# Regrouping the first expert's matmuls by batch, and one weight transfer issued ahead of the last values

## Chip, cores, metric

One core of one Trainium2 chip runs the whole program. The metric is the device time of one execution in microseconds (us). "Before" is the tuned kernel, "after" the kernel with the change; every experiment was timed beside runs of the kernel before on the same chip (e1 to e8 on one chip, e9 and e10 on a second, e11 on a third). The engines go by their short names: PE does the matmuls (TensorE), ACT is ScalarE, DVE is VectorE, POOL is GpSimd, SPq the queue of the transfers that SyncE issues.

## The reference

A gated linear attention (4 batches, 8 heads, 768 steps, head size 48) feeds a mixture of four experts whose outputs are summed with the router's weights:

```python
for t in range(S):
    state = f[:, :, t, :, None] * state + k[:, :, t] (outer) v[:, :, t]
    y[:, :, t] = q[:, :, t] @ state
x = y as (batch * seq, heads * head_dim)            # 3072 x 384
for e in range(4):
    out += p[:, e:e+1] * (relu(x @ w1[e]) @ w2[e])  # w1 384x1024, w2 1024x384
```

## The kernel before

The 768 steps are cut into six chunks of 128; a chunk has 4 batches x 128 = 512 rows for the experts. Attention of the next chunk runs between the expert matmuls of this one. Nobody wrote the order of the instructions. The kernel describes each step as an `Op` with a cost, dependencies, a rank (`prio`, lower goes first) and the buffers it takes and frees. At build time a list scheduler, `Plan.run`, gives each free engine the best-ranked step that is ready, in a modelled time. Each engine then gets its instructions in the planned order and executes them in that order.

```python
rooms = {"ps_m": 4, "ps_t": 4, ..., "e": 3, ...}     # buffers of each kind; ps_* are PSUM banks, which matmuls write

def run(self):                                        # cut
    while left:
        for e in ("PE", "ACT", "DVE", "POOL", "DMA"):
            while free_at[e] <= now + 1e-9:
                # first step by rank that is ready and whose buffers are free
                ...
                for k in o.frees:
                    self.left[k] -= 1
                    if self.left[k] == 0:
                        freeing.append((o.end + self.LATENCY, k[0], self.slot[k]))
```

Three steps play a part later: the exponentials write the tile `e` (three buffers); for chunks after the first a small transfer `egs` copies one row of it elsewhere, and `e` is free once this copy and two products have read it; and loads for the chunk after next compete with transposing transfers (`tp`) on one queue.

```python
GS.append(P.add(f"egs {c}.{b}", {"POOL": 0.8}, on(dma_egs), s(10), deps=[ex], takes=[("egs", c, b)],
                frees=[("e", c, b)], lag=2.8) if c and more else None)
...
et = [P.add(f"tp {c}.{b}", {"DMA": 1.8}, on(dma_tp), s(4), deps=[qm, km], ...)]
...
add_load(c + 2, nm, 2 * half, 2, u0 + {0: 38}.get(c, 30) + 4 * half + j, deps=wd[3, 1])
...
if c == 0:                                            # expert 0 of the first chunk
    for fcs in (range(KF // 2), range(KF // 2, KF)):
        for n0, n1, xs in ((0, N2, LO), (N2, NT, HI)):
            zip_units([x for x in hl(c, 0, n0, n1, xs) if x[2] in fcs], [])
```

Of the kernel before, what the change touches and what calls it, by code (L numbers as in the profile page):

```python
# [102 lines left out]
def kernel(  # L103
# [11 lines left out]
    nc = tc.nc  # L115
    B, H, S, D = q.shape
    assert (B, H, S, D) == (4, 8, 768, 48)
    T = 128
# [6 lines left out]
    KD = Din // 128  # L125
    KF = F // 128
    NT = B * T
    N2 = NT // 2
# [11 lines left out]
    P = Plan(rooms)  # L140
# [18 lines left out]
    for i in range(rooms["e"]):  # L159
# [5 lines left out]
        out=mask01, in_=mask01, compare_op=ALU.is_ge, fill=0.0,  # L165
# [15 lines left out]
    w1_sb = wpool.tile([128, E, KD, F], BF16)  # L181
# [18 lines left out]
    def tl(kind, *key):  # L200

        if (kind, key) not in tiles:
            room = kind if kind in rooms else "ps_m" if kind in ("hp", "op", "pp") else "ps_t"
            slot = P.slot[(room, kind) + key if room.startswith("ps_") else (room,) + key]
            if room in ("gp", "qk", "e"):
                tiles[kind, key] = pads[room, slot]
            else:
                shape, dt = shapes[kind]
                pool = ps if room.startswith("ps_") else wk
                tiles[kind, key] = pool.tile(shape, dt, name=f"{room}{slot}")  # L210
        return tiles[kind, key]

    def after(later, earlier):
        tc.add_manual_dep(later.ins, earlier.ins.name,
                          mybir.DependencyInfo(mybir.DependencyClass.Sync, mybir.DependencyReason.DATA),
                          reason="order of transfers")
# [4 lines left out]
    def hh(b, n=1):  # L221
        return slice((b % 2) * H, (b % 2 + n) * H)
# [8 lines left out]
    def load(c, nm, b, n):  # L231
        if (c, nm) == (0, "v"):
            ins[c, nm, b] = nc.gpsimd.dma_start(out=tl("vb", c, b), in_=srcs[nm][c, :, b * H:(b + n) * H, :])  # L233
            if b < 2:
                after(ins[c, nm, b], ins[v_gate[b]])
            return
        ins[c, nm, b] = nc.sync.dma_start(out=tl(nm, c, b // 2)[:, hh(b, n), :],  # L237
                                          in_=srcs[nm][c, :, b * H:(b + n) * H, :])
        if (c, nm, b) == (1, "f", 0):
            after(ins[c, nm, b], ins["w", 6])  # L240
        if (c, nm, b) == (1, "f", 1):
            after(ins[c, nm, b], ins["w", w_gate])

    def load_w(i, e, which, ks, cols):
        w, r = (w1_sb, w1_r) if which == 1 else (w2_sb, w2_r)
        ins["w", i] = nc.gpsimd.dma_start(out=w[:, e, ks, cols], in_=r[e][:, ks, cols])  # L246
        if i == w_last:
            after(ins["w", i], ins[1, "k", 0])
# [115 lines left out]
        for kk in range(ks.start, ks.stop):  # L364
            nc.tensor.transpose(out=tl("xp", c, b, ks.start)[:, kk, :], in_=tl("yb", c, b)[:, kk * 128:(kk + 1) * 128], identity=ident)  # L365

    def mm_h(c, e, fc, n0, n1):
        for kk in range(KD):
            nc.tensor.matmul(out=tl("hp", c, e, fc, n0)[:, n0:n1], lhsT=w1_sb[:, e, kk, fc * 128:(fc + 1) * 128],  # L369
                             rhs=tl("xT", c)[:, kk, n0:n1], start=(kk == 0), stop=(kk == KD - 1))  # L370

    def half_of(c, n0):
        return n0 // N2 if c == 1 else 0

    def relu(c, e, fc, n0, n1, eng):
        dst, src = tl("h", c, e, half_of(c, n0))[:, fc, n0:n1], tl("hp", c, e, fc, n0)[:, n0:n1]
        if eng == "DVE":
            nc.vector.tensor_relu(out=dst, in_=src)  # L378
        else:
            nc.scalar.activation(out=dst, in_=src, func=AF.Relu)  # L380
# [21 lines left out]
    ld = {}  # L402
    def add_load(c, nm, b, n, prio, deps=(), cost=None):
        op = P.add(f"ld {nm}{c}.{b}", {"DMA": cost or (1.05 if c else 1.1) * n}, lambda e: load(c, nm, b, n), prio,
                   deps=deps, takes=[(nm, c, b // 2)], lag=2.0)
        for i in range(n):
            ld[c, nm, b + i] = op
        return op


    v_gate = [(0, "k", 1), (0, "k", 2)]
    for i, x in enumerate("f0 k0 q0 f1 k1 q1 f2 f3 k2 q2 v0 k3 q3 v1 v2 v3".split()):
        nm, b = x[0], int(x[1])
        if nm == "v":
            iss = P.add(f"v issue {b}", {"POOL": 0.8}, lambda _, b=b: load(0, "v", b, 1), -600 + b,
                        deps=[vi, ld[v_gate[min(b, 1)]]] if b else [ld[v_gate[0]]], takes=[("vb", 0, b)], lag=1.2)
            vi = iss
            ld[0, "v", b] = P.add(f"ld v0.{b}", {"DMA": 1.1}, lambda _: None, -1000 + i, deps=[iss], lag=2.0)
        else:
            add_load(0, nm, b, 1, -1000 + i)  # L420

# [4 lines left out]
    w_last, w_gate = len(pieces) - 1, len(pieces) - 3  # L426
    wd = {}
    for i, (e, which, ks, cols) in enumerate(pieces):
        if i == 7:
            add_load(1, "f", 0, 1, -454.5, deps=wd[2, 1], cost=0.1)  # L430
        if i == w_last:
            for x in ((1, "f", 1, 1), (1, "k", 0, 2), (1, "q", 0, 2), (1, "v", 0, 2)):
                add_load(*x, -430 + len(ld), deps=wd[3, 1])
        iss = P.add(f"w issue {i}", {"POOL": 0.8}, lambda _, i=i, x=(e, which, ks, cols): load_w(i, *x),
                    -500 + i, deps=[vi] + ([ld[1, "k", 0]] if i == w_last else []))
        op = P.add(f"w {i}", {"DMA": 2.25 if i < 6 else 4.5}, lambda _: None, -400 if i == w_last else -460 + i, deps=[iss], lag=1.5)
        wd[e, which] = wd.get((e, which), []) + [op]
    for x in ((1, "f", 2, 2), (1, "k", 2, 2), (1, "q", 2, 2), (1, "v", 2, 2)):
        add_load(*x, -400 + len(ld), deps=wd[3, 1])

# [95 lines left out]
    unit = [0]  # L536
    hdone, omm, oev = {}, {}, {}

    def add_h(c, e, fc, n0, n1, xs):
        p, n = unit[0], n1 - n0  # L540
        key = ("ps_m", "hp", c, e, fc, n0)
        m = P.add(f"h {c}.{e}.{fc}.{n0}", {"PE": 0.645 * n / NT}, lambda _: mm_h(c, e, fc, n0, n1), p,
                  deps=[wd[e, 1][fc * len(wd[e, 1]) // KF]] + [t for b in xs for t in xdone[c, b]], takes=[key], lag=0.2, frees=[("xT", c)])
        hdone[c, e, fc, n0] = P.add(f"relu {c}.{e}.{fc}.{n0}",
                                    {"ACT": 0.6, "DVE": 0.69} if n == NT else {"ACT": 0.39, "DVE": 0.42},
                                    lambda g: relu(c, e, fc, n0, n1, g), p - 3, deps=[m],
                                    takes=[("h", c, e, half_of(c, n0))], frees=[key])

    def add_o(c, e, nt, half):
        p = unit[0] + 0.5  # L550
# [20 lines left out]
    ALL, LO, HI = list(range(B)), [0, 1], [2, 3]  # L571

    def zip_units(hs, os):
        for i in range(max(len(hs), len(os))):
            if i < len(hs):
                add_h(*hs[i])
            if i < len(os):
                add_o(*os[i])
            unit[0] += 1

    def hl(c, e, n0, n1, xs):
        return [(c, e, fc, n0, n1, xs) for fc in range(KF)]

    def ol(c, e, nts):
        return [(c, e, nt, half) for nt in nts for half in range(2)]

    for c in range(C):
        u0 = unit[0]
        if c + 1 < C:
            base = u0 + {0: 10, 1: 0}.get(c, -6)  # L590
            attention(c + 1, lambda b, s, base=base: base + 2 + 5 * b + s, 2)
        if c + 2 < C:
            for half in range(2):
                for j, nm in enumerate("fkqv"):
                    add_load(c + 2, nm, 2 * half, 2, u0 + {0: 38}.get(c, 30) + 4 * half + j, deps=wd[3, 1])
        if c == 0:
            for fcs in (range(KF // 2), range(KF // 2, KF)):
                for n0, n1, xs in ((0, N2, LO), (N2, NT, HI)):
                    zip_units([x for x in hl(c, 0, n0, n1, xs) if x[2] in fcs], [])
        elif c == 1:  # L600
            zip_units([], ol(0, E - 1, ALL))
            zip_units(hl(c, 0, 0, N2, LO), [])
            for e in range(1, E):
                zip_units(hl(c, e, 0, N2, LO), ol(c, e - 1, LO))
            zip_units(hl(c, 0, N2, NT, HI), ol(c, E - 1, LO))
            for e in range(1, E):
                zip_units(hl(c, e, N2, NT, HI), ol(c, e - 1, HI))
            zip_units(hl(c + 1, 0, 0, NT, ALL), ol(c, E - 1, HI))
        elif c == 2:
            pass  # L610
        else:
            zip_units(hl(c, 0, 0, NT, ALL), ol(c - 1, E - 1, ALL))
        for e in range(E if c == 1 else 1, E):
            zip_units(hl(c, e, 0, NT, ALL), ol(c, e - 1, ALL))
# [3 lines left out]
    done = P.run()  # L618
# [45 lines left out]
```

## Time and profile before

| | before |
|---|---|
| time, median | 298.27 us (three runs, 298.17 to 299.92) |
| span of the profiled run | 296.4 us |
| PE waits from 25 us to the end | none |

The chain and PE's timeline around 20 us stand in the prediction.

### The profile page before, as it was taken

What the parts mean: (1) busy time and instruction counts of PE and PEld (TensorE: products, weight loads), DVE (VectorE), ACT (ScalarE), POOL (GpSimd) and SP (SyncE); (2) the same over time, 40 slices, a digit from 0 to 9 for tenths busy, and PEclk for the clock granted to TensorE, in tenths of its full rate; (3) what the DMA queues carried; (4) which work ended last, traced back from release to release, by engine and by line L of the source; (5) the groups of instructions that cost most, each with busy time, mean ns of one, the idle gap of its engine ahead of it and who ended that gap; (6) DMA issues with size and microseconds to landing.
All of it is one profiled execution on the core that took longest, in us unless ns stands there. A gap on an engine that the chain in (4) does not pass through costs nothing.

```text
span 296.4 us, 5570 instructions
## 1 busy us (share of the span) xinstructions
PE 289.8 (98%) x2161; PEld 170.7 (58%) x2161; DVE 127.8 (43%) x251; ACT 173.3 (58%) x318; POOL 107.8 (36%) x182
## 2 busy tenths in 40 slices
PE   7999999999999999999999999999999999999995
PEld 2467555567777775555555555555555555555553
DVE  6776012695674673055365435243523222101223
ACT  5757556757674677777475565554475544465440
POOL 5787201338578259145448372243220000000000
PEclk9999999999999999999999999999999999999999
DMA  7999999998989969996989942102521100200002
GB/s 149 201 154 206 207 194 197 182 200 184 189 174 193 183 136 203 206 209 119 196 163 209 175 96 32 29 0 67 123 59 31 27 2 27 80 2 0 0 2 106
DMA packets 136462, 36.43 MB, mean 123 GB/s; under 512 B 126812, under 2 KB 135644, under 8 KB 136436
## 3 DMA queue, kind: packets, MB, share of 16 engines
q1 hardware_dynamic: 125188, 29.35, 48.9%
q0 software_dynamic: 11248, 6.72, 16.5%
q8 instruction: 17, 0.28, 0.4%
q14 instruction: 9, 0.07, 0.1%
HBM read 31.51 MB, written 4.72 MB: 122 GB/s over the span
## 4 chain that ended last, share of the span: by engine, by line
PE 91%; DMA 4%; SPq 2%; POOL 1%; issue 0%; DVE 0%
PE ps_m L384 42%; PE ps_m L369 42%; DMA w_sb<-in_moe_w_dram 2%; SPq L237 2%; PE ps_t L325 2%; DMA k<-in_k_dram 1%; PE ps_t L340 1%; PE ps_t L336 1%; PE ps_t L346 1%; PE ps_t L273 1%; POOL vb L233 1%; PE ps_t L310 0%; POOL w_sb L246 0%; DVE o L391 0%; PE ps_t L365 0%
## 5 line engine op out<-in xcount | busy, mean ns | idle before, releaser
L380 ACT ACTIVATE h<-ps_m 128x512 bf16<-128x512 f32 (+1 forms) x191 | 101.9, 539 | 92.5 <-PE ps_m L369 89.1
L369 PE MATMUL ps_m<-xT,w_sb 128*128 128x512 bf16 (+1 forms) x696 | 152.1, 342 | 0.5 <-DMA w_sb<-in_moe_w_dram 0.5
L384 PE MATMUL ps_m<-w_sb,h 128*128 128x384 bf16 (+1 forms) x776 | 151.5, 324 | 0.0
L384 PEld LDWEIGHTS <-h 128*128 128x128 bf16 x776 | 75.1, 98 | 58.6
L391 DVE SCALAR_TENSOR_TENSOR o<-ps_m,pn,o 128x384 f32<-128x384 f32 (+1 forms) x73 | 44.6, 612 | 109.6 <-PE ps_m L384 103.3
L369 PEld LDWEIGHTS <-w_sb 128*128 128x128 bf16 x696 | 65.5, 98 | 43.3 <-DMA w_sb<-in_moe_w_dram 0.9
L301 POOL TENSOR_TENSOR qk<-q,e 128x384 bf16<-128x384 f32 x18 | 21.5, 1198 | 34.7 <-ACT e L293 32.4
L329 DVE TENSOR_TENSOR AT<-ps_t,mask 128x512 bf16<-128x512 f32 x48 | 29.9, 682 | 5.8 <-PE ps_t L325 5.8
L360 POOL TENSOR_TENSOR Sf<-Sf,egs 48x192 f32<-48x192 f32 x40 | 20.1, 501 | 33.1 <-DVE Sf L353 31.0
L293 ACT ACTIVATE e<-ps_t 128x384 f32<-128x384 f32 x48 | 26.7, 667 | 4.7 <-PE ps_t L273 3.5
L378 DVE TENSOR_SCALAR h<-ps_m 128x256 bf16<-128x256 f32 (+1 forms) x41 | 20.4, 508 | 19.0 <-PE ps_m L369 14.8
L301 POOL TENSOR_TENSOR qk<-k,e 128x384 bf16<-128x384 f32 x20 | 20.2, 1013 | 7.7 <-ACT e L293 4.4
L353 DVE TENSOR_TENSOR Sf<-Sf,ps_t 48x192 f32<-48x192 f32 x40 | 14.0, 350 | 10.9 <-PE ps_t L346 10.2
L246 POOL DMA_DIRECT2D w_sb<-in_moe_w_dram x11 | 8.8, 808 | 20.3 <-DMA k<-in_k_dram 19.0
L361 POOL CAST sb<-Sf 48x192 bf16<-48x192 f32 x40 | 13.6, 339 | 2.6
L393 ACT ACTIVATE o<-ps_m,pn 128x384 f32<-128x384 f32 x22 | 12.8, 581 | 2.8 <-PE ps_m L384 1.7
L629 PE MATMUL ps_m<-busy 128*128 128x512 bf16 x35 | 11.9, 449 | 1.5 <-DVE busy L144 1.5
L298 POOL DMA_DIRECT2D egs<-e x16 | 9.0, 564 | 7.7 <-ACT e L293 7.7
L265 ACT ACTIVATE ex<-f 128x768 f32<-128x768 f32 (+1 forms) x14 | 10.4, 745 | 2.1 <-DMA f<-in_f_logit_dram 2.0
L340 PE MATMUL ps_t<-vb,AT 128*128 128x48 bf16 x192 | 11.5, 184 | 0.0
L228 POOL CAST vb<-v 128x384 bf16<-128x384 f32 x18 | 9.7, 561 | 4.0 <-DMA v<-in_v_dram 3.8
L226 ACT CAST yb<-ps_t 128x384 bf16<-128x384 f32 (+1 forms) x14 | 6.5, 464 | 7.5 <-PE ps_t L340 7.3
(54 smaller groups left out, 126.7 us busy)
## 6 DMA issues: line engine op xcount, KB each, us to landing
out_dram<-o SPq DMA_DIRECT2D x23, 192.0 KB, 2.0
w_sb<-in_moe_w_dram POOLq DMA_DIRECT2D x5, 768.0 KB, 19.2
k<-in_k_dram SPq DMA_DIRECT2D x10, 384.0 KB, 5.4
q<-in_q_dram SPq DMA_DIRECT2D x10, 384.0 KB, 5.2
v<-in_v_dram SPq DMA_DIRECT2D x10, 384.0 KB, 5.3
f<-in_f_logit_dram SPq DMA_DIRECT2D x9, 384.0 KB, 5.0
w_sb<-in_moe_w_dram POOLq DMA_DIRECT2D x6, 384.0 KB, 9.0
f<-in_f_logit_dram SPq DMA_DIRECT2D x6, 192.0 KB, 3.7
```

The lines of the kernel that those rows point to most:

```text
L293: nc.scalar.activation(out=o, in_=i, func=AF.Exp, scale=1.0 if j else -1.0)
L301: engines[eng].tensor_tensor(out=tl("qk", c, b)[:, j, :, 0:D].rearrange("t (i r) d -> t i r d", r=2), in0=tl("qk"[j], c, b // 2)[:, hh(b), ...
L329: nc.vector.tensor_tensor(out=tl("AT", c, b)[:, r].rearrange("s i t -> s (i t)"), in0=tl("A", c, b, r).rearrange("s i t -> s (i t)"), in1= ...
L340: nc.tensor.matmul(out=y[:, h * D:(h + 1) * D], lhsT=AT[:, r, i, :], rhs=vb[:, h, :], start=(c == 0), stop=True, skip_group_check=True)
L353: nc.vector.tensor_tensor(out=Sf[rows, b], in0=Sf[rows, b], in1=KV[rows, :, r, :], op=ALU.add)
L360: nc.gpsimd.tensor_tensor(out=Sf[rows, b], in0=Sf[rows, b], in1=eg, op=ALU.mult)
L361: nc.gpsimd.tensor_copy(out=nb[rows, b, :, r * D:(r + 1) * D], in_=Sf[rows, b])
L369: nc.tensor.matmul(out=tl("hp", c, e, fc, n0)[:, n0:n1], lhsT=w1_sb[:, e, kk, fc * 128:(fc + 1) * 128], rhs=tl("xT", c)[:, kk, n0:n1], sta ...
L378: nc.vector.tensor_relu(out=dst, in_=src)
L380: nc.scalar.activation(out=dst, in_=src, func=AF.Relu)
L384: nc.tensor.matmul(out=tl("op", c, e, nt, part)[:, cols], lhsT=tl("h", c, e, half_of(c, nt * T))[:, fc, nt * T:(nt + 1) * T], rhs=w2_sb[:, ...
L391: nc.vector.scalar_tensor_tensor(out=o, in0=op, scalar=pe, in1=o, op0=ALU.mult, op1=ALU.add)
```

## The change

The intent is to give PE expert work earlier in the first 25 us: batch 2 no longer waits for batch 3, and the first weight piece no longer stands behind the values of batch 3. An F tile is 128 of the 1024 hidden columns of an expert. The diff, cut to its core (helpers that pass the number of F tiles in a bank, `nf`, are left out, and lines are shortened at `...`):

```diff
+    def hp(c, e, fc, n0, n1, nf):
+        return tl("hp", c, e, fc, n0)[:, 0:nf * (n1 - n0)].rearrange("p (f n) -> p f n", f=nf)
...
+    def add_v(b, prio):                       # issue of one batch's values, chained to the issue before it
+        issued.append(P.add(f"v issue {b}", ...))
-    for i, x in enumerate("f0 k0 q0 f1 k1 q1 f2 f3 k2 q2 v0 k3 q3 v1 v2 v3".split()):
+    for i, x in enumerate("f0 k0 q0 f1 k1 q1 f2 f3 k2 q2 v0 k3 q3 v1 v2".split()):
...
         iss = P.add(f"w issue {i}", ...)
+        issued.append(iss)
+        if i == 0:
+            add_v(B - 1, -459.5)              # values of batch 3 only after weight piece 0
...
         if c == 0:
-            for fcs in (range(KF // 2), range(KF // 2, KF)):
-                for n0, n1, xs in ((0, N2, LO), (N2, NT, HI)):
-                    zip_units([x for x in hl(c, 0, n0, n1, xs) if x[2] in fcs], [])
+            for fcs, n0, n1, xs, nf in ((range(0, KF // 2), 0, N2, LO, 1), (range(0, KF // 2, 2), N2, NT - T, [2], 2),
+                                        (range(KF // 2, KF), 0, NT - T, LO + [2], 1), (range(0, KF, 4), NT - T, NT, [3], 4)):
+                zip_units([(c, 0, fc, n0, n1, xs, nf) for fc in fcs], [])
+            unit[0] = u0 + 2 * KF
```

More of the change, by code (lines that the diff above doesn't have):

```diff
@@ L365, in pe_xt, with mm_h, relu @@
             nc.tensor.transpose(out=tl("xp", c, b, ks.start)[:, kk, :], in_=tl("yb", c, b)[:, kk * 128:(kk + 1) * 128], identity=ident)
-    def mm_h(c, e, fc, n0, n1):
-        for kk in range(KD):
-            nc.tensor.matmul(out=tl("hp", c, e, fc, n0)[:, n0:n1], lhsT=w1_sb[:, e, kk, fc * 128:(fc + 1) * 128],
-                             rhs=tl("xT", c)[:, kk, n0:n1], start=(kk == 0), stop=(kk == KD - 1))
+    def hp(c, e, fc, n0, n1, nf):
+        return tl("hp", c, e, fc, n0)[:, 0:nf * (n1 - n0)].rearrange("p (f n) -> p f n", f=nf)
+    def mm_h(c, e, fc, n0, n1, nf):
+        for f in range(nf):
+            for kk in range(KD):
+                nc.tensor.matmul(out=hp(c, e, fc, n0, n1, nf)[:, f], lhsT=w1_sb[:, e, kk, (fc + f) * 128:(fc + f + 1) * 128],
+                                 rhs=tl("xT", c)[:, kk, n0:n1], start=(kk == 0), stop=(kk == KD - 1))
     def half_of(c, n0):
         return n0 // N2 if c == 1 else 0
-    def relu(c, e, fc, n0, n1, eng):
-        dst, src = tl("h", c, e, half_of(c, n0))[:, fc, n0:n1], tl("hp", c, e, fc, n0)[:, n0:n1]
+    def relu(c, e, fc, n0, n1, nf, eng):
+        dst, src = tl("h", c, e, half_of(c, n0))[:, fc:fc + nf, n0:n1], hp(c, e, fc, n0, n1, nf)
         if eng == "DVE":
@@ L408, in add_load @@
         return op
-    v_gate = [(0, "k", 1), (0, "k", 2)]
-    for i, x in enumerate("f0 k0 q0 f1 k1 q1 f2 f3 k2 q2 v0 k3 q3 v1 v2 v3".split()):
+    v_gate, issued = [(0, "k", 1), (0, "k", 2)], []
+    def add_v(b, prio):
+        issued.append(P.add(f"v issue {b}", {"POOL": 0.8}, lambda _: load(0, "v", b, 1), -600 + b,
+                            deps=issued[-1:] + ([ld[v_gate[b]]] if b < 2 else []), takes=[("vb", 0, b)], lag=1.2))
+        ld[0, "v", b] = P.add(f"ld v0.{b}", {"DMA": 1.1}, lambda _: None, prio, deps=issued[-1:], lag=2.0)
+    for i, x in enumerate("f0 k0 q0 f1 k1 q1 f2 f3 k2 q2 v0 k3 q3 v1 v2".split()):
         nm, b = x[0], int(x[1])
         if nm == "v":
-            iss = P.add(f"v issue {b}", {"POOL": 0.8}, lambda _, b=b: load(0, "v", b, 1), -600 + b,
-                        deps=[vi, ld[v_gate[min(b, 1)]]] if b else [ld[v_gate[0]]], takes=[("vb", 0, b)], lag=1.2)
-            vi = iss
-            ld[0, "v", b] = P.add(f"ld v0.{b}", {"DMA": 1.1}, lambda _: None, -1000 + i, deps=[iss], lag=2.0)
+            add_v(b, -1000 + i)
         else:
@@ L434 @@
         iss = P.add(f"w issue {i}", {"POOL": 0.8}, lambda _, i=i, x=(e, which, ks, cols): load_w(i, *x),
-                    -500 + i, deps=[vi] + ([ld[1, "k", 0]] if i == w_last else []))
+                    -600 + 3 * i, deps=issued[-1:] + ([ld[1, "k", 0]] if i == w_last else []))
         op = P.add(f"w {i}", {"DMA": 2.25 if i < 6 else 4.5}, lambda _: None, -400 if i == w_last else -460 + i, deps=[iss], lag=1.5)
+        issued.append(iss)
         wd[e, which] = wd.get((e, which), []) + [op]
+        if i == 0:
+            add_v(B - 1, -459.5)
     for x in ((1, "f", 2, 2), (1, "k", 2, 2), (1, "q", 2, 2), (1, "v", 2, 2)):
@@ L537, with add_h @@
     hdone, omm, oev = {}, {}, {}
-    def add_h(c, e, fc, n0, n1, xs):
-        p, n = unit[0], n1 - n0
+    def add_h(c, e, fc, n0, n1, xs, nf=1):
+        p, n = unit[0], (n1 - n0) * nf
         key = ("ps_m", "hp", c, e, fc, n0)
-        m = P.add(f"h {c}.{e}.{fc}.{n0}", {"PE": 0.645 * n / NT}, lambda _: mm_h(c, e, fc, n0, n1), p,
+        m = P.add(f"h {c}.{e}.{fc}.{n0}", {"PE": 0.645 * n / NT}, lambda _: mm_h(c, e, fc, n0, n1, nf), p,
                   deps=[wd[e, 1][fc * len(wd[e, 1]) // KF]] + [t for b in xs for t in xdone[c, b]], takes=[key], lag=0.2, frees=[("xT", c)])
-        hdone[c, e, fc, n0] = P.add(f"relu {c}.{e}.{fc}.{n0}",
-                                    {"ACT": 0.6, "DVE": 0.69} if n == NT else {"ACT": 0.39, "DVE": 0.42},
-                                    lambda g: relu(c, e, fc, n0, n1, g), p - 3, deps=[m],
-                                    takes=[("h", c, e, half_of(c, n0))], frees=[key])
+        done = P.add(f"relu {c}.{e}.{fc}.{n0}",
+                     {"ACT": 0.6, "DVE": 0.69} if n == NT else {"ACT": 0.5, "DVE": 0.56} if n > N2 else {"ACT": 0.39, "DVE": 0.42},
+                     lambda g: relu(c, e, fc, n0, n1, nf, g), p - 3, deps=[m],
+                     takes=[("h", c, e, half_of(c, n0))], frees=[key])
+        for f in range(nf):
+            hdone[c, e, fc + f, n0] = done
     def add_o(c, e, nt, half):
```

## The prediction

> **What bounds the kernel now.** I read the page first. TensorE (PE) is busy 289.8 of 296.4 us, so only two things can shorten the run: less PE work, or less time in which PE waits or runs filler. I then read the chain of waits in order of time, to see where PE first becomes the whole chain.
>
> ```profile
> 14.55 0.70 POOL w_sb L246
> 15.25 7.25 DMA w_sb<-in_moe_w_dram
> 22.50 0.05 issue
> 22.54 0.50 PE ps_m L369 x3
> 23.04 0.34 PE ps_t L346 x8
> 23.38 0.66 PE ps_m L369 x6
> ...
> 25.03 4.24 PE ps_m L369 x30
> 29.27 1.30 PE ps_m L384 x8
> ```
>
> The columns are start, duration, what. Up to 22.50 the chain is a weight transfer; from 22.54 to the end it is PE. The list of PE's waits from 25 us to the end is empty. So the end moves by as much as the work that PE still has to do at about 22.5 us shrinks, or as that moment moves, and by nothing else. Which weight transfer is it? The timeline of PE around it:
>
> ```profile
> 18.76 0.36 PE L340 MATMUL ps_t<-vb,AT 128*128 128x48 bf16 x8
> 18.96 1.02 PE L629 MATMUL ps_m<-busy 128*128 128x512 bf16 x4
> 19.87 0.34 PE L365 MATMUL ps_t<-ident,yb 128*128 128x128 bf16 x3
> 20.05 0.36 PE L340 MATMUL ps_t<-vb,AT 128*128 128x48 bf16 x8
> 20.67 1.16 PE L369 MATMUL ps_m<-xT,w_sb 128*128 128x256 bf16 x9 [0.26 <-DMA w_sb<-in_moe_w_dram]
> 21.66 0.33 PE L365 MATMUL ps_t<-ident,yb 128*128 128x128 bf16 x3
> 21.83 0.49 PE L369 MATMUL ps_m<-xT,w_sb 128*128 128x256 bf16 x3
> 22.54 0.50 PE L369 MATMUL ps_m<-xT,w_sb 128*128 128x256 bf16 x3 [0.22 <-DMA w_sb<-in_moe_w_dram]
> ```
>
> Here L629 is filler (keeps PE active), L340 forms a batch's attention output y, L365 transposes it, L369 is the first MoE layer. At 20.67 PE waits for weight piece 0 (expert 0, F tiles 0 to 3); 12 matmuls (four F tiles by three K steps on batches 0 and 1) follow, and at 22.54 it waits again, for piece 1 (F tiles 4 to 7). Asking for each issue alone gave the landings: value transfers of batches 1, 2, 3 issued at 11.85, 12.8 and 13.7 landed near 15.5, 17.9 and 18.4; piece 0, issued at 14.5, took 6.1 us (20.6); piece 1, issued at 15.3, took 7.2 us (22.5); the next ones landed 1.9 to 2.0 us apart. The DMA engines show a busy share of one or more throughout, so this queue is limited by transfer, not by issue.
>
> **What the Trainium skill says.** "DMA: Bandwidth & Descriptors", section "Queues, rings and completion order", says that each DMA engine consumes one ring's descriptors in order, but that completion is not FIFO over the engines. The landings agree roughly: all in issue order, though batches 2 and 3 landed 0.5 us apart and batches 1 and 2 2.4 us apart, so what one transfer costs the next isn't a constant. "TensorE: Matmul & The Clock Gate", section "Back-to-back issue gap", gives about 81 ns per matmul at N=128 in a stream that loads weights each time, against 56 ns isolated. The new kernel has such a stream, so it matters. This trace decides for 56: transposes with a new 128x128 stationary operand each go at 0.45/8 = 56 ns,
>
> ```profile
> 56.84 0.45 PE ps_t L310 x8
> ```
>
> and the 256-column matmuls at 0.66/6 = 110 ns. "PSUM — Partial Sum Buffer", section "The four PSUM rules", allows a matmul output up to one bank, 512 fp32 columns, and warns of two accumulation groups open at once in it. Four groups of 128 columns fill a bank exactly and here run one after the other, so I expect right results. The trace of before can only show a whole bank written by one 512-column matmul.
>
> **The change part by part.** (a) *Splitting expert 0 of chunk 0.* Before: 48 matmuls of 256 columns in the order F 0-3 on batches 0,1; F 0-3 on 2,3; F 4-7 on 0,1; F 4-7 on 2,3 (readiness reorders this). After, in order of priority: F 0-3 on batches 0,1 (12 of 256 columns); F 0-3 on batch 2, two F tiles a bank (12 of 128); F 4-7 on batches 0-2 (12 of 384); all F on batch 3, four F tiles a bank (24 of 128). Columns are the same: 48x256 = 12288 = 12x256 + 36x128 + 12x384. Time before: 48x0.110 = 5.28 us. After: 12x0.110 + 36x0.056 + 12x0.162 (1.30 us for eight 384-column ones above) = 1.32 + 2.02 + 1.94 = 5.28. No PE work is saved or added.
>
> (b) *What becomes possible before piece 1.* The transposed batch 2 is in SBUF at 20.73 (a copy on ACT, 20.25 for 0.48), batch 3 only at about 22.4. Before, batch 2 was tied to batch 3, so PE could do only 1.32 us of MoE work before piece 1. After, it can add F 0-3 on batch 2: 12x0.056 = 0.67 us. That is the gain, if it fits in before 22.5.
>
> (c) *Piece 0 before the values of batch 3.* It is issued one place earlier, 0.86 us, and no longer stands behind that transfer. I put what it gains at 0.5 to 0.9 us: 0.5 is the distance of the landings of batches 2 and 3, 0.9 the issue spacing. It should land at 19.7 to 20.1. Batches 0 and 1 are transposed and copied by 19.44 (18.96 + 0.48), so the weights still decide, and the first MoE matmul starts near 19.9 instead of 20.67.
>
> Does it fit? From 19.9: 1.32 + 0.67 us MoE, 0.17 the transposes of batch 2, 0.20 y of batch 3, sum 2.36: done at about 22.3, just before piece 1. If piece 0 gains only 0.3 us, PE runs to about 22.7 and 0.2 us of the 0.67 is lost.
>
> (d) *The price.* Values of batch 3 land behind piece 0, about 20.5 instead of 18.4. Its y ran at 20.05 after the mask product of 18.68 + 1.29 = 19.97; now it waits for the values, and comes to about 21.2. Its copy, transposes and second copy took from 20.41 to 22.4, about 2.0 us, so batch 3 is ready near 23.3 instead of 22.4. The first use in the new order is after F 4-7 on three batches, 22.5 + 1.94 = 24.4: hidden with 1.1 us to spare. The four state matmuls groups (L346, 0.67 us in sum) and the router's probabilities, which wait for batch 3 too, move by the same; GpSimd's state updates end at 31.9 and the next chunk's attention is at 53 or later.
>
> (e) *Evictions.* Before, 16 of 256 columns at 384 ns on ACT or 425 on DVE; after, 4 of 256, 2 of 256 (two tiles), 4 of 384 (estimate 0.5, between 384 and 597 ns), 2 of 512 at 597: about 5.5 us instead of 6.2, on engines with idle time. One of the four MoE banks is held by the router's transposes until the probabilities are made. With three banks and a cycle of about 0.28 + 0.2 + 0.39 + 0.1 = 1.0 us (estimates of handover), a bank comes free each 0.33 us, which is just the 0.33 us of a 256-column tile. I count up to 0.1 us for this.
>
> Piece 1's own landing moves by nothing: the same bytes are before it in the queue. From 22.5 on PE has 0.67 us less to do. Sum: -0.67 + 0.1 = about -0.6 us, which is 298.27 - 0.6 = 297.7.
>
> **The rivals.** *One: the full shift.* If the first MoE matmul starts 0.8 us or more earlier and everything moves with it, the end gains 0.8 to 1.2: 297.1 to 297.5. Against it: piece 1 is the chain's transfer and isn't moved. *Two: a stall at y of batch 3.* PE takes its list in order. If that y stands ahead of MoE work that is ready while its values come late, PE sits idle up to about 0.5 us, and the gain goes to between 0 and 0.3: 298.0 to 298.3. For it: before, y was issued ahead of the first MoE matmul; against it: the planner expects the values a microsecond later too, and should place it after three or four tiles. *Three: the order of later work shifts.* The kernel orders all engines' instructions from a plan made at build; a small shift early may bring another order, with a late piece or a bank wait somewhere after 30 us. With PE never waiting after 25 us there is slack (e.g. PE alternated between two experts), but I can't bound it from this trace: 298.3 to 299.3. *Four: no gain*, as piece 1 still gates the chain and batch 2 isn't placed before it: 298.3.
>
> **Range and chances.** The main line and the first rival give 297.1 to 297.8, two and four 298.0 to 298.3, three a tail above. Three runs of before spread from 298.17 to 299.92, two of them 0.1 apart. I take 297.7 with 296.9 to 298.6. Two per cent is 6.0 us; all PE time without MoE work before 20.67 that the change can touch is about 1.5 us, so faster by 2% is all but excluded, and slower by 2% needs a broken order.
>
> **What would show it.** In PE's timeline: the first L369 group at 19.7 to 20.1, 12 matmuls of 128 columns before 22.5, a last wait for a weight piece still near 22.5, and the first L384 or the end of expert 0 some 0.6 us earlier relative to before. y of batch 3 (last L340 of the first chunk) at about 21.2 behind a wait for values or MoE work. Transfers: piece 0 ahead by 0.5 to 0.9 us, values of batch 3 near 20.5. PE's total busy time should drop by filler only. Wrong would be: 128-column matmuls at 80 ns (adds 0.9 us), piece 1 landing at another time, or PE waits after 25 us.

## More of the kernel before

The granted clock is the share of its full clock that PE is given.

The page of the kernel before, its first part (busy us, share of the span, instructions) and from its second the granted PE clock in 40 slices (9 is 90% or more):

```profile
PE 289.8 (98%) x2161; PEld 170.7 (58%) x2161; DVE 127.8 (43%) x251; ACT 173.3 (58%) x318; POOL 107.8 (36%) x182
...
PEclk9999999999999999999999999999999999999999
```

From 25 us on PE is never without work, and its granted clock is 90% or more in every slice.

## The result, and the profile after

The kernel after takes 302.81 us in the median of four runs (302.50 to 303.44), before 298.58 us in the same rounds (298.17 to 299.92). A ratio here is the mean time of one kernel's fast runs over that of the other's of the same rounds, so not quite the ratio of the medians: 1.0136, interval 1.0099 to 1.0174. The change costs about 4 us, and the outputs are right.

**The first 40 us went nearly as foreseen.** PE's timeline after; the columns are start, duration, engine, line, operation, output and inputs, shapes, count, and in brackets the idle time before. L374 is the first expert layer, L340 the attention output y of batch 3:

```profile
19.26 0.81 PE L644 MATMUL ps_m<-busy 128*128 128x512 bf16 x3
19.90 0.82 PE L374 MATMUL ps_m<-xT,w_sb 128*128 128x256 bf16 x6
...
21.38 0.36 PE L340 MATMUL ps_t<-vb,AT 128*128 128x48 bf16 x8
21.59 0.83 PE L374 MATMUL ps_m<-xT,w_sb 128*128 128x128 bf16 x12
...
22.62 1.14 PE L374 MATMUL ps_m<-xT,w_sb 128*128 128x384 bf16 x6
```

The first expert matmul is at 19.90 instead of 20.67, y of batch 3 at 21.38, the twelve 128-column matmuls stand before 22.5. The last wait for a weight piece, foreseen near 22.5, is gone. To see what that is worth, count matmuls: 32 of the second layer and 24 of 512 columns of the first, beside all of expert 0, are done at 37.54 before and at 36.98 after. PE is 0.56 us ahead. Loads land at other times in each execution, so one pair of profiles is thin evidence; but at this same point the seven profiled kernels with the new start stand at 36.61 to 37.46 us (37.13 in the mean), and the three with the old start (before, e2, e9) at 37.54 to 37.60. The lead is some 0.45 us.

**The loss comes 20 to 60 us later.** The list of PE's waits from 25 us on, empty before (columns: who waited, for whom, us in total, times, longest):

```profile
PE ps_m L374 <- ACT h L385: 2.4, 1, 2.4
PE ps_t L325 <- ACT QK L226: 0.7, 1, 0.7
PE ps_m L389 <- ACT h L385: 0.4, 1, 0.4
```

The largest is here in PE's timeline after:

```profile
92.83 0.82 PE L374 MATMUL ps_m<-xT,w_sb 128*128 128x256 bf16 x6
96.08 1.30 PE L374 MATMUL ps_m<-xT,w_sb 128*128 128x256 bf16 x9 [2.43 <-ACT h L385]
97.18 1.48 PE L389 MATMUL ps_m<-w_sb,h 128*128 128x384 bf16 x4
```

PE waits 2.43 us for an eviction on ACT (the copy that empties a PSUM bank) to give a bank back. After it the matmuls are slow: four of 384 columns take 1.48 us where the same group takes 0.81 elsewhere. The table by stretches (the numbers ahead of "DMA share" and GB/s, the last two, give the granted clock) shows why. After, and below it the second stretch in the kernel before:

```profile
92.00:96.00 4.00, 1.65 (x14) 1.14 (x12) 1.07 (x3) 1.40 (x4) 2.67 (x5) 1.00 1.30 139
96.00:100.00 4.00, 3.92 (x19) 2.39 (x19) 0.42 (x1) 1.40 (x5) 3.16 (x5) 0.62 0.60 154
```

```profile
96.00:100.00 4.00, 4.00 (x45) 2.94 (x43) 2.47 (x5) 2.71 (x7) 0.00 (x0) 1.00 0.89 160
```

The granted clock is 0.62 in the four microseconds after the wait (in finer stretches 0.50 from 96.9 to 100.3 us), where before it is 1.00. In the chain, the four groups from 96.08 to 100.53 us that ran slowly take 1.30 + 1.28 + 0.64 + 1.23 = 4.45 us. The same four groups after the same wait in e9, where the clock stayed at 1.00, take 1.14 + 0.65 + 0.33 + 0.65 = 2.77, so the low clock cost 1.68 us in this execution.

**Why was ACT late?** Its timeline after, at the moment in question; L293 is the exponentials of chunk 2, L385 the evictions:

```profile
90.42 0.38 ACT L385 ACTIVATE h<-ps_m 128x256 bf16<-128x256 f32 x1 [0.59 <-PE ps_m L374]
94.60 1.16 ACT L293 ACTIVATE e<-ps_t 128x384 f32<-128x384 f32 x2 [3.79 <-DMA egs<-e]
95.65 0.65 ACT L385 ACTIVATE h<-ps_m 128x256 bf16<-128x256 f32 x2
```

ACT stood 3.79 us at an exponential whose buffer `e` was still being read by the small transfer, and PE's evictions stood behind it. In the kernel before, ACT runs the same exponentials without such a wait:

```profile
87.33 2.26 ACT L293 ACTIVATE e<-ps_t 128x384 f32<-128x384 f32 x4 [0.16 <-PE ps_t L273]
```

The transfer was issued by GpSimd at 90.42 us after, and at 76.67 before. First the line of before, then that of after:

```profile
76.67 0.54 POOL L298 DMA_DIRECT2D egs<-e  x1 [3.84 <-ACT e L293]
```

```profile
90.42 0.58 POOL L298 DMA_DIRECT2D egs<-e  x1
```

So a transfer came 14 us later because the first 25 us were reordered. Going back along the exponentials to the gates' load, one finds the first difference in the queue of loads. Before, then after:

```profile
68.47 0.39 SPq L237 DMA_DIRECT2D f<-in_f_logit_dram  x1
69.70 3.35 SPq L314 DMA_TRANSPOSE QK<-qk  x2
```

```profile
69.08 1.34 SPq L314 DMA_TRANSPOSE QK<-qk  x1
70.48 0.56 SPq L237 DMA_DIRECT2D f<-in_f_logit_dram  x1
71.20 2.29 SPq L314 DMA_TRANSPOSE QK<-qk  x1
```

One transposing transfer has overtaken the load of chunk 2's gate inputs, which is issued at 70.48 instead of 68.47. The first exponentials of chunk 2 then move from 75.52 to 80.43 on ACT, and GpSimd, whose order puts products and state updates ahead of it, issues the small transfer 10 us after that.

In sum for the profiled runs: 2.43 + 0.67 + 0.40 = 3.50 us of waits, 1.68 of low clock, less 0.56 gained, is 4.6; the spans differ by 301.7 - 296.4 = 5.3. The remaining 0.7 us I do not assign. (The profiled execution after was the slowest of the four; by the medians the change costs 4.2 us.)

### The profile page after: what moved, and what is told of

Same layout as the page of the kernel before. It is cut to its first block, busy times and chain, and to the rows that moved or that the text cites. A ratio compares the mean times of both kernels' runs of the same rounds, so it can differ in the third digit from the quotient of the medians.

```text
span 301.7 us, 5587 instructions
## 1 busy us (share of the span) xinstructions
PE 290.9 (96%) x2172; PEld 170.7 (57%) x2172; DVE 124.0 (41%) x245; ACT 175.7 (58%) x321; POOL 106.9 (35%) x181
## 4 chain that ended last, share of the span: by engine, by line
PE 84%; DMA 5%; POOL 3%; SPq 3%; issue 1%; ACT 1%; DVE 1%; POOLq 0%; ACTq 0%
PE ps_m L389 38%; PE ps_m L374 38%; DMA q<-in_q_dram 4%; SPq L237 2%; POOL qk L301 2%; PE ps_t L325 2%; PE ps_t L340 1%; DMA egs<-e 1%; PE ps_t L336 1%; PE ps_t L346 1%; PE ps_t L273 1%; SPq L314 1%; POOL Sf L360 1%; PE ps_t L310 1%; ACT QK L226 1%
## 5 line engine op out<-in xcount | busy, mean ns | idle before, releaser
L385 ACT ACTIVATE h<-ps_m 128x512 bf16<-128x512 f32 (+2 forms) x193 | 104.5, 547 | 87.7 <-PE ps_m L374 84.3
L374 PE MATMUL ps_m<-xT,w_sb 128*128 128x512 bf16 (+3 forms) x708 | 152.4, 340 | 2.4 <-ACT h L385 2.4
L374 PEld LDWEIGHTS <-w_sb 128*128 128x128 bf16 x708 | 65.5, 98 | 46.9 <-issue 3.3
L293 ACT ACTIVATE e<-ps_t 128x384 f32<-128x384 f32 x48 | 26.9, 667 | 10.5 <-PE ps_t L273 5.4
L360 POOL TENSOR_TENSOR Sf<-Sf,egs 48x192 f32<-48x192 f32 x40 | 20.1, 502 | 34.0 <-DVE Sf L353 31.8
L383 DVE TENSOR_SCALAR h<-ps_m 128x256 bf16<-128x256 f32 (+1 forms) x35 | 16.9, 492 | 29.3 <-PE ps_m L374 18.4
L644 PE MATMUL ps_m<-busy 128*128 128x512 bf16 x34 | 10.9, 423 | 1.5 <-DVE busy L144 1.5
L340 PE MATMUL ps_t<-vb,AT 128*128 128x48 bf16 x192 | 11.5, 184 | 0.0
L269 ACT ACTIVATE gp<-ex 128x768 bf16<-128x768 f32 (+1 forms) x14 | 10.5, 750 | 0.3
L340 PEld LDWEIGHTS <-AT 128*128 128x128 bf16 x192 | 9.9, 97 | 1.3
```

Source lines behind the costliest of these rows:

```text
L293: nc.scalar.activation(out=o, in_=i, func=AF.Exp, scale=1.0 if j else -1.0)
L340: nc.tensor.matmul(out=y[:, h * D:(h + 1) * D], lhsT=AT[:, r, i, :], rhs=vb[:, h, :], start=(c == 0), stop=True, skip_group_check=True)
L360: nc.gpsimd.tensor_tensor(out=Sf[rows, b], in0=Sf[rows, b], in1=eg, op=ALU.mult)
L374: nc.tensor.matmul(out=hp(c, e, fc, n0, n1, nf)[:, f], lhsT=w1_sb[:, e, kk, (fc + f) * 128:(fc + f + 1) * 128], rhs=tl("xT", c)[:, kk, n0: ...
L383: nc.vector.tensor_relu(out=dst, in_=src)
L385: nc.scalar.activation(out=dst, in_=src, func=AF.Relu)
```

## The experiments

**Theory.** The new start is a gain; the loss comes from the different order that the plan makes of later work, set off by one swap of two transfers. **Rivals.** The new start itself costs (transfers, PSUM banks); or the late values cost; or the wait near 94 us has another cause than the buffer.

| run | what it is | median us | ratio to before, 95% interval |
|---|---|---|---|
| e1_graft | start of after, later order of before | 297.37 | 0.9972, 0.9956 to 0.9988 |
| e2_ungraft | start of before, later order of after | 304.11 | 1.0184, 1.0155 to 1.0213 |
| e3_split_only | regrouping alone, planned anew | 302.56 | 1.0133, 1.0113 to 1.0153 |
| e4_weight_only | weight piece ahead alone, planned anew | 298.23 | 1.0003, 0.9986 to 1.0020 |
| e5_f2_first | after, gates' load ranked ahead | 298.62 | 1.0014, 0.9994 to 1.0033 |
| e6_e4 | after, four `e` buffers | 299.26 | 1.0035, 1.0019 to 1.0051 |
| e7_egs_landing | after, `e` planned free at landing | 298.95 | 1.0021, 1.0006 to 1.0037 |
| e8_fill | after, filler in the wait | 301.60 | 1.0106, 1.0087 to 1.0126 |
| e9_plan_nudge | before, one planned cost changed | 302.63 | 1.0150, 1.0125 to 1.0174 |
| e10_f2_at | e5 and one PE step moved | 298.85 | 1.0012, 0.9989 to 1.0034 |
| e11_graft_split | start of e3, later order of before | 298.44 | 1.0000, 0.9977 to 1.0022 |

All gave correct outputs. Before had medians of 298.27 (e1 to e4), 298.23 (e5 to e8), 298.12 (e9, e10, on a second chip) and 298.45 (e11, on a third).

**e1_graft and e2_ungraft: start and later order exchanged.** The kernel carries a list of the other kernel's plan from the end of expert 0 on, and gives out buffers anew (the code is put in short):

```diff
     done = P.run()
+    later = [by[name, i] for e, name, i in LATER]     # the other kernel's order and engines
+    done = [o for o in done if o not in later] + later
+    # buffers handed out again, first freed first, along this order
```

> The changed kernel's first 30 us (all of the first chunk's expert 0), then every engine's order of the kernel before, instruction for instruction. Theory (the start gains some 0.56 us, the loss comes from the order that the plan makes of later work): 297.7 to 298.1 us beside 298.3 of before, no wait of PE over 1 us after 25 us, clock 1.00 throughout. Rival (the new start itself costs, e.g. by the transfers' or PSUM banks' timing): 301 us or more, as the changed kernel.

> The reverse: the first 30 us of the kernel before, then the changed kernel's order. Theory: the loss follows the later order, 302 to 304 us, with a PE wait of 2 us or more on an ACT eviction near 94 us. Rival (the new start costs): about 298.3.

e1 took 297.37 us, 0.28% less than before (0.84 us of 298.3), and its list of PE's waits from 21 us on is empty. e2 took 304.11 us, just above the 302 to 304 expected, with PE's wait on an ACT eviction grown to 3.5 us. The theory holds on both sides: **the start of the change is a gain, its later order the whole loss.** e1 also came out a little below the range I gave. In its profile PE reaches the point counted above at 37.29 us against 37.54 before, and the span is 0.3 us shorter: what this start gained is kept to the end. It is the version that beats both kernels.

**e3_split_only and e4_weight_only: which half brings the order.** Each half of the diff alone, planned anew.

> Only the regrouping of expert 0; values and weights issued as before. Theory: the regrouping alone makes the plan put the second transpose-transfer of the first chunk pair before the load of the next gates, so it has the slow later order: 302 to 304 us. Rival (the weight piece ahead of the values upsets the transfers): about 298.3.

> Only the weight piece ahead of the last values; expert 0 grouped as before. Theory: its plan keeps the order of before around 70 to 100 us: 297.8 to 298.5 us, the first MoE matmul near 19.9 us but little of it kept, since half of the work is tied to the late batch 3. Rival (the values' delay is what costs): 300 us or more.

e3 has the slow order (302.56 us, PE waits 2.2, 0.7 and 0.4 us as after). e4 keeps the order of before around the swap, and its time, so the late values do not cost. Two of its lines show that it gained nothing at the start in the profiled execution. The first is in PE's timeline, the second in the list of PE's waits from 21 us on:

```profile
20.54 0.83 PE L374 MATMUL ps_m<-xT,w_sb 128*128 128x256 bf16 x6 [0.18 <-DMA w_sb<-in_moe_w_dram]
```

```profile
PE ps_t L365 <- DVE yb L228: 0.5, 1, 0.5
```

In that execution PE started at 20.54 and then stood 0.5 us for batch 3, whose values come late. (The loads that all this waits for land at other times in each execution: GpSimd's first gated value issue was at 11.85 before, 11.27 after, 12.63 in e4. The start near 19.9 that I expected did not come, and this one profile does not tell how much of that the late loads did.)

**e5_f2_first: undo the swap.**

```diff
-  u0 + {0: 38}.get(c, 30) + 4 * half + j, deps=wd[3, 1])
+  20 if (c, half, j) == (0, 0, 0) else u0 + {0: 38}.get(c, 30) + 4 * half + j, deps=wd[3, 1])
```

> The changed kernel with one number altered: the load of chunk 2's first gates gets a higher rank than the transposing transfer that overtook it, and the plan is made anew. Theory (that one swap of two transfers starts the slow order): exponentials of chunk 2 and their small transfers early again, no ACT wait on the small transfer near 94 us, 297.2 to 298.6 us. Rival (the order would be slow whichever of the two goes first): over 300.

298.62 us: one rank gives back most of the loss. Against before in the same rounds 0.4 us is left, of the 4.2 of the kernel after. The only wait of PE left after 21 us is the one of 0.7 us near 59 us. The time lies just above the range I expected, as that wait stayed.

**e9_plan_nudge: cause the swap in the kernel before.** Nothing of the change is in it; one cost in the plan is altered, the instructions are the same in number and size.

```diff
-  {"POOL": 1.1}
+  {"POOL": 0.7 if (c, b) == (1, 2) else 1.1}
```

> The kernel before with nothing of the change; only one estimate in its plan is altered, a GpSimd product of chunk 1 counted as 0.7 instead of 1.1 us, so that the transposing transfer is ready just in time to overtake the load of chunk 2's gates. Theory (that overtaking is what the change set off): 301.5 to 303 us, with PE's wait of 2 to 3.5 us on an ACT eviction near 94 us; no 0.7 us wait near 59 us, as that part of the order stays. Rival (the slow order needs the changed start): 298 to 299.

302.63 us. The list of its waits:

```profile
PE ps_m L369 <- ACT h L380: 3.4, 1, 3.4
PE ps_m L384 <- ACT h L380: 0.4, 1, 0.4
```

A nudge of the plan could have changed more than the swap. The plans rule that out: the first place in which any engine's order in e9 differs from before is this swap (at 72.85 us of the plan's time), and from the swap on every engine's order in e9 is that of after. With e5 this shows the swap, with the order that the plan makes behind it, to be enough to cause the loss in this kernel and needed for it. The 0.7 us wait near 59 us isn't there, so that one belongs to the regrouped start's plan and not to the swap.

**e6_e4 and e7_egs_landing: the buffer.** A fourth buffer, or a plan that counts the third one honestly:

```diff
- rooms = {... "e": 3, ...}
+ rooms = {... "e": 4, ...}                                              # e6
- freeing.append((o.end + self.LATENCY, k[0], self.slot[k]))
+ freeing.append((o.end + self.LATENCY + (o.lag if o.name.startswith("egs") else 0.0), k[0], self.slot[k]))   # e7
```

> The changed kernel with a fourth buffer for the exponentials' tile; the late order of transfers stays. Theory (PE's 2.4 us wait is ACT's wait for a buffer of three that a small transfer still reads, and the clock falls because of that wait): that wait and the clock drop gone, the 0.7 and 0.4 us waits stay: 298.2 to 299.6 us. Rival (ACT is late for another reason, as GpSimd's lateness): 301 or more.

> The changed kernel, but the plan counts that buffer as free only when the small transfer has landed (2.8 us more), as the chip does. It then places the last exponentials after two more evictions. Theory (the plan's optimistic release put an ACT instruction ahead of evictions that PE needs): PE's wait at 94 us under 1 us, 298.4 to 300.3 us. Rival (the wait moves on with the exponentials): 301.5 to 303.

Both keep the late small transfer and both lose the 2.4 us wait and the low clock (granted 0.999 and 1.000 in the profiled runs): 299.26 and 298.95 us. In e7, ACT's timeline shows the same exponentials, now behind the evictions:

```profile
92.98 0.38 ACT L385 ACTIVATE h<-ps_m 128x256 bf16<-128x256 f32 x1 [0.59 <-PE ps_m L374]
94.22 1.19 ACT L293 ACTIVATE e<-ps_t 128x384 f32<-128x384 f32 x2 [0.86 <-DMA egs<-e]
```

So the swap and the late transfer did little harm by themselves; ACT's place in line for its buffer did. The plan freed `e` when the transfer had been issued; the chip had it free when it had landed, 2.9 to 4.1 us after the issue for this kind of transfer (5.1 us for the one that ACT waited for in e2).

**e8_fill: what the clock costs.**

```diff
+        if o.name == "h 1.0.6.256":                   # the matmul that waits
+            idle = ps.tile([128, 512], FP32, name="ps_t0")
+            for _ in range(11):
+                nc.tensor.matmul(out=idle, lhsT=busy[:, 0:128], rhs=busy, start=True, stop=True)
```

> The changed kernel with 11 filler matmuls of 512 columns (11 x 0.216 = 2.4 us) into a bank idle at that time, ahead of the matmul that waits near 94 us. Theory (the wait lets the clock fall to half for some 4 us, 2 us lost beside the wait itself): clock 1.00 throughout, the wait under 0.3 us but the next MoE matmul at the same moment, 300.5 to 301.3 us. Rival (the clock falls for another reason or costs nothing): 302.3 to 303.5.

301.60 us, a little over my range. That is below the kernel after by 1.2 us by the medians and 0.9 by the ratios, but the two intervals overlap, so the times alone do not show the saving. ACT's 3.8 us wait is unchanged and the next expert matmul comes as late as before, but at full clock:

```profile
93.96 2.54 PE L648 MATMUL ps_t<-busy 128*128 128x512 bf16 x11
96.59 1.14 PE L374 MATMUL ps_m<-xT,w_sb 128*128 128x256 bf16 x9
97.57 0.81 PE L389 MATMUL ps_m<-w_sb,h 128*128 128x384 bf16 x4
```

The group of four takes 0.81 us again. What ties the low clock to PE's wait is the count over all runs: a mean clock of 0.993 or 0.994 is in 11 of the 21 executions of the kernels with the long wait (after, e2, e3, e9), and in none of the 42 of the other experiments, which have 0.998 or more. In after, e2, e3 and e9 the executions with it are longer than those without by 0.5, 1.8, 1.1 and 1.1 us.

The length of the wait does not decide. The profiled e2 and e9 waited longer than after, 3.45 and 3.43 us, at a clock of 1.00 throughout. Their traces suggest what does: where the clock changes between 25 us and the end (after, e3), it does so at whole multiples of 3.41 us from its first record, and it is then 0.50 for one such stretch. In after and e3 the idle 2.43 and 2.23 us lie wholly in the stretch before that; in e2 and e9 a boundary would cut them into 1.45 + 2.00 and 1.38 + 2.05. That is a reading of four executions; no run tested it.

**e10_f2_at: the wait of 0.7 us.** From e5, with one PE step (scores of chunk 1's second batch) placed after the first matmuls of expert 3's second layer.

```diff
+    late = next(o for o in done if o.name == "at 1.1")
+    done.remove(late)
+    done.insert(1 + next(i for i, o in enumerate(done) if o.name == "o 0.3.0.0"), late)
```

> As e5_f2_first, and in PE's order the scores of chunk 1's second batch stand behind the first matmuls of expert 3's second layer. Theory (those matmuls have their weights by 58.3 us and can fill the 0.7 us in which PE waits for ACT's copy): that wait gone, 297.7 to 298.2 us, 0.4 to 0.7 below e5. Rival (they wait for something else, or the wait moves on): 298.4 or more.

298.85 us, no gain to be seen: my expectation failed, and its rival was right that the wait moves on. (The intervals alone would still allow the 0.4 us expected over e5; the waits are 0.6 us in place of 0.7.) Its list of waits:

```profile
PE ps_t L340 <- DVE AT L329: 0.4, 1, 0.4
PE ps_t L336 <- DVE AT L329: 0.2, 1, 0.2
```

The scores, moved back, reached DVE's mask product later, and PE waited for that instead.

**e11_graft_split: which half brings the gain.** As e1, with the start of e3.

> As e1_graft (later order of the kernel before), but the first 30 us are those of e3: the regrouping without the weight piece ahead of the values. It divides e1's gain of 0.84 us. Theory (the regrouping lets PE work on batch 2 while it waits for piece 1, which is most of the gain, and the earlier piece 0 makes room for it): 297.6 to 298.0 us, a gain of 0.3 to 0.6 us. Rival (the earlier weight piece is what counts): 298.1 to 298.4, no gain.

Ratio 1.0000: no gain in the mean, so this expectation was not met, though the interval still allows a gain of up to 0.7 us. PE's timeline in it:

```profile
21.05 1.16 PE L1493 MATMUL ps_m<-xT,w_sb 128*128 128x256 bf16 x9 [0.72 <-DMA w_sb<-in_moe_w_dram]
...
22.21 1.16 PE L1493 MATMUL ps_m<-xT,w_sb 128*128 128x256 bf16 x15
...
23.72 1.14 PE L1493 MATMUL ps_m<-xT,w_sb 128*128 128x384 bf16 x6
```

Once batch 2 is a group of its own, PE runs from piece 0 on without a second wait; piece 1 no longer binds, but piece 0 is as late as ever. With piece 0 early and the old grouping (e4) PE stands for batch 3. Only both together show a gain clear of noise, 0.84 us in e1. How it divides stays open: the profile of e3, which has the same start as e11, is at the point counted above at 37.10 us, 0.4 ahead of before, and e11 at 37.56, as their first expert matmuls came at 20.59 and 21.05, each behind its wait for piece 0.

## Why the prediction was wrong, point by point

- **What bounds the kernel (right for an unchanged order only).** I wrote that the end moves with PE's work at about 22.5 us "and by nothing else". In e1, with the later order of before, that holds: what PE is ahead at 37 us (0.25 in its profile) is in the span (0.3). With the order that the plan made, it does not.
- **Part (a) (right).** No PE work was added: the twelve 128-column matmuls take 0.67 us in the chain, 56 ns each.
- **Part (c) (right start, by luck).** Piece 0 landed at 13.1 + 5.7 = 18.8 us in the profiled run after, ahead of the 19.7 to 20.1 foreseen, in part because that execution's loads came 0.6 us earlier than in before. So the weights did not decide: filler did, which the chain has at 19.42 for 0.65 us and which outlasted the copy of batch 1 (done at 19.73), and the start of 19.90 met the forecast for another reason.
- **Part (d) (right).** Values of batch 3 landed at 19.8 (foreseen 20.5), y ran at 21.38 (21.2); the delay stayed hidden. The 0.1 us counted in (e) for PSUM banks does not show: PE waits for no bank between 20 and 30 us after.
- **Part (b) (about right in size, wrong in reason).** I took piece 1 for the bound and 0.67 us of batch 2's matmuls for the gain. Piece 1 landed at 21.5 us after and at 22.2 in e1, and its first matmuls stand at 22.62 and 22.94: it no longer binds. PE runs on from an earlier start, and everything moves with it. That is my first rival, which I had put aside because piece 1 isn't moved; its 297.1 to 297.5 has e1's 297.37 in it. The sum of -0.6 us stands against -0.84 measured in e1, whose interval goes from -0.4 to -1.3 and so tells neither from the other by the number.
- **The third rival: the step that failed.** I wrote that PE's lack of waits after 25 us shows slack, and gave a new later order 298.3 to 299.3, at most 1 us. My own sign of being wrong, waits of PE after 25 us, came. The list of waits of before shows only that this order has none; it says nothing of how another order would do. The runs showed 302.8: one swapped pair of transfers, worth some 4 us of the time whether the change is there (e5) or not (e9), by way of a buffer that the plan frees too early (e6, e7), and a clock that in about half of the executions fell after PE's wait. I could have asked how near the planned order was to other orders: the diff shows that each rank and each time of the first chunk enters the one plan from which everything later is made.
- **Open.** The 0.7 us wait near 59 us belongs to the regrouped start's plan (it is in e3, e5 and after, not in e9); e10 only moved it on. The share of each half of the change in e1's gain, and 0.7 us of the 5.3 between the profiled runs, are not assigned.

## What to carry to other kernels

Where a scheduler makes the instruction order at build time, a local change is a change of the whole order: compare the orders first (which transfer, which buffer comes in another place), and to learn what the change itself is worth, graft the old order onto the new start as in e1. A plan should count a buffer as free when the chip has it free, above all behind a transfer; a release planned 3 us early lay dormant in the kernel before and cost some 3.5 us here (e7 against after, each beside before) as soon as the transfer came late. A wait on PE can cost more than its length, because the clock may fall after it.

## What the Trainium skill lacked or had wrong

- "TensorE: Matmul & The Clock Gate", section "What's actually happening", gives an idle window of about 3.4 us before the clock halves. Here 2.43 us without a matmul (2.23 in e3) was followed by a granted clock of 0.62 over four microseconds, while 3.45 us in e2 and 3.43 in e9 were followed by 1.00. It came in some executions and not in others (mean clock 0.994 in three of four runs of after, 0.999 in one), and with filler in the gap it was 1.00 (e8).
- The same page, section "Back-to-back issue gap", gives about 81 ns per matmul at 128 columns in a stream that loads weights each time. Twelve such matmuls took 0.67 us here, 56 ns each, which is its figure for the isolated gap. Its 131 ns at 512 columns was not reached either: 15 such matmuls took 3.24 us in the chain of before, 216 ns each, again its isolated figure.
- "DMA: Bandwidth & Descriptors", section "Anatomy of one DMA — SWDGE (gpsimd) path", gives about 2.0 us of fixed time per transfer. The 2 KB copies from SBUF to SBUF took 2.9 to 4.1 us from issue to landing between 60 and 100 us of the run after (5.1 us for one in e2), while other transfers were under way; no page gives a figure for that case, on which e7's fix depends.
